# Batch 0's second half of G inside its first FFN steps, batch 1's expert search at step 24, and a plan adapted to both

## The chip, the cores and the metric

One core of one Trainium2 chip. The metric is the device time of one launch in microseconds, median over runs. The core has TensorE for matmuls (PE in the profile, its weight loads PEld), VectorE (DVE), ScalarE (ACT), GpSimd (POOL), and SyncE (SP), whose queue issues nearly all DMA transfers of this kernel. Each engine works through its own queue in order.

## What is computed

Eight batches, eight heads, 576 tokens per batch, head width 64. A packed attention comes first: 32 queries p attend to k and v, and the 32 packed rows then serve as keys and values for q. The output, 4608 rows of 512, goes through a mixture of eight experts, where each row takes its best expert:

```
p_packed = softmax(p k^T / 8) v             # 32 rows per head
x        = softmax(q p_packed^T / 8) p_packed   # rows of 8 heads side by side: 4608 x 512
e        = argmax(x w_gate)                 # per row
out[row] = softmax(x w_gate)[e] * sigmoid(x w_output_gate)[e] * (relu(x w1[e]) w2[e])
```

All arrays are float32. For the inputs drawn, the rows of a batch go to one expert but for a few.

## The kernel before, in words

The kernel works batch by batch, and per batch on one expert, which it finds at run time from the packed rows. Rows that belong to another expert are mended afterwards (`first_leftover`, and a loop that runs zero times here if nothing is left).

For batch b there are five jobs, each a Python generator that emits instructions piece by piece:

- `encode(b)`: scores of p against k on PE (`ps_s`), their maximum (`nm` on DVE; from batch 1 on a relay between ACT and DVE, `top_of`), exponentials on ACT, transposes on DVE, the product with v on PE (`ps_pp`), the packed rows (`ppc`, stored to `pp_d`), their transpose `ppT`, the expert's scores (`ps_e`), and last `find_top`, which leaves the expert's number in `estar_i`. 18 pieces for batch 0, 16 for the others.
- `weights(b)`: SP loads the expert's number into a register (`value_load`) and issues four 512 KB transfers of w1 (tile `w`, line 505); the next piece issues four of w2 (`wst`); then, in turn for each of the four parts of w2, ACT makes a rounded copy `w2h` (L519) and DVE or POOL the remainder `w2l` (L521).
- `values_up(b)`: G = packed rows times w1 on PE (`ps_G`, L99), so that the FFN's first product can be taken from the attention weights directly. G comes in two halves of 512 columns; each half needs two of w1's four parts. A half's PSUM banks are split into `Gh` (ACT, L83) and `Gl` (DVE, L84), for batch 0 in quarters of 256 columns.
- `route(b)`: scores of q against the packed rows (`ps_s2T`), softmax over the packed rows (DVE, ACT, POOL), the attention weights as `ah` (ACT) and `al` (DVE or POOL), stored to `a_d`, then the gate: per-row expert, scale `scm_all`, and a count of the rows that need mending (`keys`).
- `ffn(b)`: yields after each step. Steps 1 to 8: eight column blocks of the first product for the first 256 tokens (`ps_h`, L92, six matmuls each), each taken out by ACT (L577) and DVE (L580) as `hT`. Steps 9 to 16: the second product for those tokens (`ps_o`, L618, twelve matmuls per two steps of work). Steps 17 to 24: the first product for the other 320 tokens. Steps 25 to 27: the second product of the last 64 tokens (L633). Steps 28 to 35: the remaining two blocks of 128 tokens. Column blocks 0 to 3 need only the first half of G. The last batch has three steps more.

Order is written out by hand. `START` is emitted before batch 0's FFN, and `PLANS[b]` says which pieces follow which step of `ffn(b)`: "24:r" puts one piece of `route(b+1)` behind step 24. Letters in capitals and `t`, `W`, `G` mean a job of batch b itself (Y encode, t route, W weights, G values_up), small letters the same job of batch b+1 (y, r, w, g), `x` is encode of batch b+2, `k`, `v`, `q` fetch the next input block, `d` scales and stores the two output blocks that batches 0 and 1 keep back, `l` is the mending, and a digit is `keep_warm`: matmuls on a blank tile. `CFG["warm"]` has their sizes in blocks of 128 columns, and `CFG["pool"]` lists the element-wise steps that go to POOL instead of DVE. An instruction that waits holds up what stands behind it in its engine's queue; SP's queue holds the value loads, all fetches and all stores.

PSUM has eight banks, four named "a" and four named "f". G's first half, `ps_h` and `ps_o` use "f" banks in rotation; a bank is given on when ACT and DVE have taken its contents. The q buffers are two, the k and v buffers six.

Of the kernel before, what the change touches and what calls it, by code (L numbers as in the profile page):

```python
# [18 lines left out]

P = 128  # L20
BANK = 512
CFG = dict(raw=6, rq=2, pa=4, w1=4, wst=4, w2=6, a1T=2, at=2, row=4, ht=4, ob=4, last=(4, 2, 3), warm=(8, 6, 1, 6, 3, 1, 5, 5),
           pool=("w2.2", "w3.3", "w4.3", "w5.3", "w6.3", "w7.3", "w3.0", "w4.0", "w5.0", "w6.0", "w7.0", "w0.0",
# [4 lines left out]

START = "kkYY3YvqYYvk1qYYkYYYY4YYYYYYtYttWt2tqttWk6v7tv5tvqttttvytGGqGG"
STEADY = ("3:yy 5:q 7:k 8:rWryy 9:rryrr 10:r 11:t 12:r 13:rr 14:ry 16:w 17:rw 18:x 19:vx 20:q 21:x 24:vx "
          "26:xrxw 28:wr 29:r 30:kww 31:xgx 33:g 34:rwwxwxg")
PLANS = ["1:W 3:k 4:WW 6:WtW 7:ty 8:W 9:Wy 10:ty 12:W 13:y 14:ttyt 15:ytyy 17:y 18:tyt 19:q 20:y 21:yrry 22:t "
# [5 lines left out]
        + [STEADY] * 4 + ["6:W 7:t 8:l 21:ll 28:l 29:l 30:l 33:l"]  # L41


@with_exitstack
def tile_packed_attn_then_moe(ctx, tc, first_in, qT, kp, k2, v, w1, w2, out):
# [26 lines left out]

    NA = CFG["pa"]

    def bank(name, tag="a"):
        return pool.tile([P, BANK], F32, tag=tag, name=name, bufs=NA if tag == "a" else 8 - NA)
# [40 lines left out]
    def keep_warm(i):  # L117

        ps = bank("warm", "fa"[0 < i < 6])
        n = CFG["warm"][i]  # L120
        while n:
# [21 lines left out]
    no_row = float(2 * B * S)  # L143
    key_i = sb.tile([P, B * T * Q * E], I32, tag="hT", name="key_i", bufs=CFG["ht"], **WIDE)
    nc.gpsimd.iota(key_i, pattern=[[1, B * T * Q * E]], base=0, channel_multiplier=0)
# [46 lines left out]
    def eng(what, *at):  # L192
        return nc.gpsimd if what + ".".join(map(str, at)) in CFG["pool"] else nc.vector

# [10 lines left out]
    def fetch(x):  # L205
# [5 lines left out]
        tag = "rq" if x == "q" else "raw"  # L211
        bufs = CFG[tag]
        if x == "v":
# [29 lines left out]
    def encode(b):  # L243
# [42 lines left out]
        for hf in range(2):  # L286
# [10 lines left out]
            yield  # L297
        a1s = [sb.tile([P, S], F32, tag="row", name="a1", bufs=CFG["row"]) for _ in range(NG)]
        ats = [sb.tile([P, S], F32, tag="a1T", name="a1T", bufs=CFG["a1T"]) for _ in range(NG)]
# [517 lines left out]
    def place(plan, b):  # L817

        kinds = dict(x=(encode, 2), y=(encode, 1), Y=(encode, 0), r=(route, 1), t=(route, 0), w=(weights, 1), W=(weights, 0),
                     g=(values_up, 1), G=(values_up, 0), l=(first_leftover, 0))  # L820
        for c in plan:
            if c in kinds:
                piece(kinds[c][0], b + kinds[c][1])
            elif c == "d":
                store()
            elif c.isdigit():
                keep_warm(int(c))
            else:
                fetch(c)

    by_hand = tc.manual_schedule()
    by_hand.__enter__()
    place(START, 0)
    for b in range(B):
        plan = {}
        for x in PLANS[b].split():
            i, what = x.split(":")
# [13 lines left out]
def _layout(q, k, v, p, moe_w_gate, moe_w_output_gate, moe_w1, moe_w2):  # L851
# [26 lines left out]
    def parts(x):  # L878
        x = x.reshape(P, -1)
        n = x.shape[1] - NPAIR * SQ  # L880
        return [x[:, :n], x[:, n:]]
    queues = dict(k=[parts(kp[0]), parts(k2[0])], v=[[v[0, 0]], [v[0, 1], w_go]], q=[parts(x) for x in qT[0]])
    order = [x for c in START if queues.get(c) for x in queues[c].pop(0)]
    return dict(
# [27 lines left out]
```

## Time and profile before

| | us |
|---|---|
| median of 3 runs | 399.0 (398.81 to 399.13) |
| the profiled execution | 400.09 |
| its span, first to last instruction | 398.5 |
| PE busy | 388.6 (98% of the span) |
| DVE, ACT, POOL busy | 257.8, 185.5, 96.5 |
| mean granted TensorE clock, share of full | 0.993 |
| moved by DMA | 83.77 MB, 210 GB/s over the span |

The profiled execution took 1.6 us more than its span and 1.1 us more than the median of the runs. PE is nearly always busy, so the reading goes to the few places where it isn't, or where what it does is not work of the reference.

### The profile page before, as it was taken

What the parts mean: (1) busy time and instruction counts of PE and PEld (TensorE: products, weight loads), DVE (VectorE), ACT (ScalarE), POOL (GpSimd) and SP (SyncE); (2) the same over time, 40 slices, a digit from 0 to 9 for tenths busy, and PEclk for the clock granted to TensorE, in tenths of its full rate; (3) what the DMA queues carried; (4) which work ended last, traced back from release to release, by engine and by line L of the source; (5) the groups of instructions that cost most, each with busy time, mean ns of one, the idle gap of its engine ahead of it and who ended that gap; (6) DMA issues with size and microseconds to landing.
All of it is one profiled execution on the core that took longest, in us unless ns stands there. A gap on an engine that the chain in (4) does not pass through costs nothing.

```text
span 398.5 us, 9681 instructions
## 1 busy us (share of the span) xinstructions
PE 388.6 (98%) x3787; PEld 311.7 (78%) x3787; DVE 257.8 (65%) x717; ACT 185.5 (47%) x424; POOL 96.5 (24%) x85
## 2 busy tenths in 40 slices
PE   8899998999999999999999999999999999999995
PEld 3468876678869786898868887798968887698875
DVE  5678677685778973567663866469564873568421
ACT  2256444562477262744565336553465343632320
POOL 3441014042026210541044012330135010620010
PEclk9899999999999999999999999999999999999998
DMA  7899079935993499324991369613861049101931
GB/s 294 320 390 383 5 224 313 404 119 211 396 318 139 152 306 400 112 97 148 330 403 45 127 211 386 246 38 108 306 251 61 2 141 375 65 29 27 356 118 53
DMA packets 35534, 83.77 MB, mean 210 GB/s; under 512 B 3486, under 2 KB 15136, under 8 KB 35488
## 3 DMA queue, kind: packets, MB, share of 16 engines
q1 hardware_dynamic: 35024, 81.89, 56.0%
q10 hardware_dynamic: 432, 1.26, 0.8%
q8 instruction: 30, 0.49, 0.5%
q14 instruction: 16, 0.13, 0.1%
q0 software_dynamic: 32, 0.00, 0.0%
HBM read 67.93 MB, written 15.27 MB: 209 GB/s over the span
## 4 chain that ended last, share of the span: by engine, by line
PE 91%; DMA 4%; DVE 2%; ACT 1%; SPq 1%; issue 1%; ACTq 0%
PE ps_o L618 43%; PE ps_h L92 25%; PE ps_o L633 8%; DMA w<-in_w_dram 4%; PE ps_G L99 3%; PE ps_pp L99 3%; PE ps_s L99 2%; PE ps_s2T L99 2%; PE warm L123 2%; PE ps_lg L99 1%; SPq L505 1%; PE ps_lo L778 0%; PE ps_lh L762 0%; DVE nm L290 0%; PE ps_ppT L336 0%
## 5 line engine op out<-in xcount | busy, mean ns | idle before, releaser
L618 PE MATMUL ps_o<-w2h,hT 128*128 128x512 f32 (+2 forms) x528 | 168.0, 390 | 0.0
L618 PEld LDWEIGHTS ps_o<-w2h,hT 128*128 128x128 f32 x528 | 98.5, 188 | 23.3 <-issue 2.8
L618 PE MATMUL ps_o<-w2l,hT 128*128 128x512 f32 (+2 forms) x264 | 101.7, 385 | 0.0
L580 DVE SCALAR_TENSOR_TENSOR hT<-ps_h,hT 128x256 fp32r<-128x256 f32 x192 | 60.6, 352 | 51.0 <-ACT hT L577 50.7
L521 POOL TENSOR_TENSOR w2l<-wst,w2h 128x1024 fp32r<-128x1024 f32 x26 | 63.9, 2467 | 112.0 <-ACT w2h L519 109.1
L92 PE MATMUL ps_h<-ah,Gh 128*128 128x256 f32 (+1 forms) x256 | 77.4, 302 | 0.5 <-DVE Gl L84 0.3
L92 PE MATMUL ps_h<-ah,Gl 128*128 128x256 f32 (+1 forms) x256 | 75.7, 296 | 0.0
L92 PE MATMUL ps_h<-al,Gh 128*128 128x256 f32 (+1 forms) x256 | 75.7, 296 | 0.0
L577 ACT ACTIVATE hT<-ps_h 128x320 fp32r<-128x320 f32 (+1 forms) x128 | 50.9, 416 | 40.9 <-PE ps_h L92 40.5
L618 PEld LDWEIGHTS ps_o<-w2l,hT 128*128 128x128 f32 x264 | 49.7, 188 | 8.7
L92 PEld LDWEIGHTS ps_h<-ah,Gh 128*128 128x128 f32 x256 | 48.6, 190 | 4.1 <-issue 1.2
L92 PEld LDWEIGHTS ps_h<-al,Gh 128*128 128x128 f32 x256 | 48.6, 190 | 0.5
L92 PEld LDWEIGHTS ps_h<-ah,Gl 128*128 128x128 f32 x256 | 48.5, 190 | 0.0
L519 ACT CAST w2h<-wst 128x1024 fp32r<-128x1024 f32 x32 | 33.7, 1061 | 14.3 <-issue 8.5
L84 DVE TENSOR_TENSOR Gl<-ps_G,Gh 128x512 fp32r<-128x512 f32 (+1 forms) x36 | 21.0, 626 | 23.9 <-ACT Gh L83 23.7
L601 ACT ACTIVATE ob<-ps_o,scm_all 128x512 f32<-128x512 f32 (+1 forms) x28 | 19.1, 681 | 33.3 <-PE ps_o L618 31.5
L436 POOL TENSOR_TENSOR al<-a2T,ah 128x576 fp32r<-128x576 f32 (+1 forms) x9 | 11.8, 1317 | 81.5 <-ACT ah L433 81.5
L633 PE MATMUL ps_o<-w2h,hT 128*128 128x512 f32 x64 | 25.8, 403 | 0.0
L633 PE MATMUL ps_o<-w2l,hT 128*64 128x512 f32 x64 | 23.8, 392 | 0.0
L83 ACT CAST Gh<-ps_G 128x512 fp32r<-128x512 f32 (+1 forms) x36 | 17.8, 544 | 7.7 <-PE ps_G L99 7.2
L304 ACT ACTIVATE a<-ps_s,nm 128x144 f32<-128x144 f32 x64 | 18.5, 408 | 4.9 <-DVE nm L273 4.8
L412 ACT ACTIVATE s<-s 128x576 f32<-128x576 f32 (+1 forms) x18 | 11.1, 631 | 20.4 <-DVE s L409 19.0
(177 smaller groups left out, 403.9 us busy)
## 6 DMA issues: line engine op xcount, KB each, us to landing
w<-in_w_dram SPq DMA_DIRECT2D x36, 512.0 KB, 5.9
wst<-in_w_dram SPq DMA_DIRECT2D x36, 512.0 KB, 9.0
vt<-in_v_dram SPq DMA_DIRECT2D x14, 650.0 KB, 10.8
q<-in_qT_dram SPq DMA_DIRECT2D x14, 576.0 KB, 5.2
out_dram<-ob SPq DMA_DIRECT2D x31, 256.0 KB, 2.0
a_d<-a2T SPq DMA_DIRECT2D x16, 320.0 KB, 2.9
k<-in_kp_dram SPq DMA_DIRECT2D x7, 640.0 KB, 8.1
k<-in_k_dram SPq DMA_DIRECT2D x7, 576.0 KB, 7.0
```

Of the source, the lines that this page charges most:

```text
L83: (hi_eng or nc.scalar.copy)(hi, src)
L84: (lo_eng or nc.vector).tensor_tensor(lo, src, f(hi), ALU.subtract)
L92: res = nc.tensor.matmul(dst, a, m, start=j == 0, stop=j == len(seq) - 1)
L99: res = nc.tensor.matmul(dst, a, m, start=j == 0, stop=j == len(seqs[0]) - 1)
L304: nc.scalar.activation(a1s[g][:, c * SQ:(c + 1) * SQ], s1[c // 2][g][:, (c % 2) * SQ:(c % 2 + 1) * SQ], AF.Exp, bias=nm[:, g, c:c + 1], sc ...
L519: nc.scalar.copy(hi, st)
L521: eng("w", b, j).tensor_tensor(lo, st, f(hi), ALU.subtract)
L577: nc.scalar.activation(hT[:, :n], ps, AF.Relu)
L580: nc.vector.scalar_tensor_tensor(hT[:, d0:d0 + s1 - s0], ps[:, s0:s1], 0.0, f(hT[:, s0:s1]), op0=ALU.max, op1=ALU.subtract)
L601: nc.scalar.activation(ob[:, cs], ps[:, cs], AF.Copy, scale=sc)
L618: nc.tensor.matmul(ps[:, cs], a, m[:, cs], start=fc == i == 0, stop=fc == FC - 1 and i == 2)
L633: nc.tensor.matmul(ps[:n], a, m, start=i == 0, stop=i == len(seq) - 1)
```

## The change

Only the plan changes: `START`, `STEADY`, the three own plans of batches 0 to 2, the plan of the last batch, the sizes of the blank matmuls, and the list of steps that go to POOL. No arithmetic changes.

- `START` ends in "GkyG" where it ended in "vytGGqGG": only the first half of G is made ahead of the FFN, with the first piece of batch 1's encode between its matmuls and its split. The second half's matmuls and split stand behind step 2 of batch 0's FFN ("2:GGW").
- In `START` the first piece of `route(0)` (the matmuls `ps_s2T`) moves ahead of the last pieces of `encode(0)`, and the transfers of w2 are issued directly behind those of w1.
- In `PLANS[0]` the last pieces of `encode(1)` (`find_top`) and the search with w1's transfers move to step 24 ("24:yyw"), from steps 29 and 30. The stores `d` move from step 26 to 23. The split of w2 moves from steps 1, 4, 6, 8, 9 and 12 to steps 2, 3, 6, 7, 9 and 10.
- In `STEADY` and the others, pieces shift by one to three steps; among them the relay of `encode(b+2)` goes from step 21 to 23. The first piece of the mending goes from step 8 to 11.
- The blank matmuls go from 8, 6, 1, 6, 3, 1, 5, 5 blocks to 7, 4, 1, 6, 1, 8, 3, 1.

```diff
-CFG = dict(raw=6, rq=2, pa=4, w1=4, wst=4, w2=6, a1T=2, at=2, row=4, ht=4, ob=4, last=(4, 2, 3), warm=(8, 6, 1, 6, 3, 1, 5, 5),
+CFG = dict(raw=6, rq=2, pa=4, w1=4, wst=4, w2=6, a1T=2, at=2, row=4, ht=4, ob=4, last=(4, 2, 3), warm=(7, 4, 1, 6, 1, 8, 3, 1),
            pool=("w2.2", "w3.3", "w4.3", "w5.3", "w6.3", "w7.3", "w3.0", "w4.0", "w5.0", "w6.0", "w7.0", "w0.0",
-                 "w1.2", "w3.2", "w4.2", "w5.2", "w6.2", "w7.2", "mul2.0.0", "sub1.0.1", "w2.1", "w1.1",
-                 "al3.0.1", "al4.0.1", "al5.0.1", "al6.0.1", "al7.0.1", "sub1.0.0", "w3.1", "w4.1", "w5.1",
-                 "w6.1", "w7.1", "al1.0.0", "w2.3", "mul0.0.0", "al0.0.1", "al2.0.0", "sub2.0.1", "sub0.0.1",
-                 "mul0.0.1", "al0.0.0", "mul1.0.1", "sub2.0.0"))
+                 "w1.2", "w3.2", "w4.2", "w5.2", "w6.2", "w7.2", "w2.1", "w1.1", "al3.0.1", "al4.0.1", "al5.0.1",
+                 "al6.0.1", "al7.0.1", "sub1.0.0", "w3.1", "w4.1", "w5.1", "w6.1", "w7.1", "al1.0.0", "al0.0.1",
+                 "sub2.0.1", "al0.0.0", "w2.3", "mul1.0.0", "sub0.0.1", "sub0.0.0", "al2.0.1", "sub2.0.0",
+                 "w0.2", "mul2.0.1", "al2.0.0", "mul0.0.0"))
-START = "kkYY3YvqYYvk1qYYkYYYY4YYYYYYtYttWt2tqttWk6v7tv5tvqttttvytGGqGG"
-STEADY = ("3:yy 5:q 7:k 8:rWryy 9:rryrr 10:r 11:t 12:r 13:rr 14:ry 16:w 17:rw 18:x 19:vx 20:q 21:x 24:vx "
-          "26:xrxw 28:wr 29:r 30:kww 31:xgx 33:g 34:rwwxwxg")
-PLANS = ["1:W 3:k 4:WW 6:WtW 7:ty 8:W 9:Wy 10:ty 12:W 13:y 14:ttyt 15:ytyy 17:y 18:tyt 19:q 20:y 21:yrry 22:t "
-         "24:r 25:r 26:d 27:yt 28:rr 29:yr 30:rw 31:wk 33:r 34:rtkgrgrg",
-         "0:Wyyy 3:W 4:W 5:vyyyyW 6:W 7:W 9:yyWyt 10:yW 11:yt 12:rtt 13:yydr 15:yrry 16:r 17:q 20:q 21:r 22:r "
-         "23:w 24:vx 25:xx 26:rwk 27:rw 28:rvr 30:rt 31:x 32:rrg 33:xrww 34:vwgxwrwg",
-         "0:ky 3:tyyy 5:Wq 6:yy 7:W 8:ryr 9:yr 10:rr 11:rkry 12:rrx 13:xxv 14:xqyrxw 16:wx 17:rx 18:rv 20:kxr "
-         "21:r 26:g 28:r 30:wg 31:gr 32:w 33:xwx 34:wwww"] \
-        + [STEADY] * 4 + ["6:W 7:t 8:l 21:ll 28:l 29:l 30:l 33:l"]
+START = "kkvYY3qYYYvYqYY1kYkYYYYY4YtYYtYtWtWtv2tqvttv7qt5tvt6ttGkyG"
+STEADY = ("3:yy 7:k 8:ryy 9:rrrrW 10:ty 11:qr 12:r 13:r 14:r 15:r 16:yw 17:rrw 18:x 19:v 21:x 23:vx 24:x 25:r "
+          "26:xwx 27:r 28:wx 29:qr 30:wkw 31:gx 33:g 34:rwxwxwg")
+PLANS = ["0:kq 1:t 2:GGW 3:W 5:ty 6:W 7:tW 9:WWW 10:yW 11:tt 12:t 13:y 14:ytyy 15:qt 16:yy 17:y 18:tty 19:y "
+         "21:ryt 22:y 23:dr 24:yyw 25:r 26:r 29:rw 30:tr 31:r 32:rt 33:rr 34:rkgkrgg",
+         "0:Wyyy 4:WW 5:yyyWy 6:vW 7:W 9:Wyyyt 10:yW 11:yt 12:t 13:rydy 15:ytr 16:ryr 17:rq 20:r 21:q 22:v "
+         "23:rwxx 24:wrx 26:kr 27:twr 28:r 29:v 31:xrx 32:rrvg 33:rrw 34:wwgxwwg",
+         "0:yk 2:q 3:ytyy 5:W 6:yy 7:W 8:ryr 9:yxr 10:k 11:rxrry 12:rr 13:rxxqv 14:xyx 16:rrxw 18:wr 20:xr "
+         "23:k 24:vr 28:g 29:r 30:rwg 31:gw 32:www 33:wxx 34:w"] \
+        + [STEADY] * 4 + ["6:W 7:t 11:l 21:ll 29:l 30:l 31:l 34:l"]
```

## Rows read from the trace of the kernel before

**Rows 1.** Idle PE time from 24 us on: who waited for whom, us, times, longest.

```profile
PE ps_G L99 <- DMA w<-in_w_dram: 1.6, 3, 1.2
PE ps_h L92 <- DVE Gl L84: 0.3, 1, 0.3
PE ps_h L92 <- DVE hT L580: 0.3, 1, 0.3
```

**Rows 2.** The chain that ended last: start us, us, what, times.

```profile
17.42 7.46 DMA w<-in_w_dram
...
26.05 0.36 ACT Gh L83
...
27.30 0.44 DVE Gl L84
...
27.88 4.54 PE ps_h L92 x36
32.42 10.90 PE ps_o L618 x48
...
54.16 3.67 PE ps_o L633 x16
...
63.45 7.58 DMA w<-in_w_dram
...
206.18 1.88 PE ps_G L99 x32
...
290.97 1.12 PE ps_o L633 x4
```

**Rows 3.** Timeline to 30 us: start, us, engine, line, operation, count [idle before, releaser].

```profile
15.30 1.20 PE L99 MATMUL ps_s2T<-q,ppT 64*32 64x288 f32 x32
...
17.53 4.38 PE L123 MATMUL warm<-blank 128*128 128x128 f32 x12 [1.03 <-issue]
...
21.83 1.24 PE L99 MATMUL ps_s<-k 64*32 64x144 f32 x64
22.24 1.79 POOL L436 TENSOR_TENSOR al<-a2T,ah 128x288 fp32r<-128x288 f32 x2 [0.43 <-ACT ah L433]
...
22.84 1.89 PE L99 MATMUL ps_G<-w,ppT 64*32 64x512 f32 x24
...
25.91 0.39 PE L92 MATMUL ps_h<-ah,Gh 128*128 128x256 f32 x1
```

**Rows 4.** DMA issues around 16.4 us, w1's second part: size, us to landing.

```profile
w<-in_w_dram SPq DMA_DIRECT2D x1, 512.0 KB, 5.0
```

**Rows 5.** Page, part 5, w2's rounded copy: count, busy us, mean ns, idle before.

```profile
L519 ACT CAST w2h<-wst 128x1024 fp32r<-128x1024 f32 x32 | 33.7, 1061 | 14.3 <-issue 8.5
```

**Rows 6.** Timeline, 56 to 82 us: batch 1's search, its G, its first FFN step.

```profile
59.95 0.56 SPq L640 DMA_DIRECT2D out_dram<-ob  x1
...
61.36 2.43 SPq L505 DMA_DIRECT2D w<-in_w_dram  x4
...
67.51 1.09 PE L99 MATMUL ps_G<-w,ppT 64*32 64x512 f32 x16
...
70.52 0.75 DVE L436 TENSOR_TENSOR al<-a2T,ah 128x576 fp32r<-128x576 f32 x1
...
72.08 0.19 PEld L618 LDWEIGHTS ps_o<-w2h,hT 128*128 128x128 f32 x1 [0.84 <-issue]
...
74.85 0.19 PEld L92 LDWEIGHTS ps_h<-ah,Gh 128*128 128x128 f32 x1 [0.23 <-issue]
```

**Rows 7.** Busy us of each engine by stretch (instructions), granted clock, DMA share, GB/s.

```profile
17.20:20.60 3.40, 3.07 (x7) 2.03 (x8) 2.89 (x9) 0.89 (x2) 0.76 (x2) 0.50 0.94 341
...
25.90:43.30 17.40, 17.14 (x104) 14.78 (x104) 14.29 (x34) 12.56 (x33) 2.86 (x3) 1.00 0.79 318
...
206.20:251.90 45.70, 45.70 (x459) 37.51 (x467) 29.64 (x83) 23.15 (x52) 11.38 (x7) 1.00 0.58 217
```

**Rows 8.** ACT's timeline in batch 5, the take-outs behind the relay.

```profile
288.05 1.09 ACT L577 ACTIVATE hT<-ps_h 128x320 fp32r<-128x320 f32 x3
```

## The prediction

> **What bounds the kernel now.** I read the waits of PE first. From 24 us on it stands idle in three places only, all before 80 us: G waits for w1's transfers, and two steps of the FFN wait for DVE [rows 1]. After that the busy time by stretch shows PE full: a whole batch of the steady plan takes 45.70 us with 45.70 us of PE [rows 7]. So PE's own work is the bound from 80 us to the end, and nothing that the change shifts there can win anything. It can win only in the start (to 26 us) and in batch 0. The chain of waits gives the unit prices: a `ps_h` matmul of 256 columns 4.54 us / 36 = 0.126, a `ps_o` matmul 10.90 / 48 = 0.227, a whole G 1.88 us when nothing holds it up, one quarter's `Gh` 0.36 and `Gl` 0.44 [rows 2].
>
> **Term 1, the search for batch 1.** G of batch 1 starts at 67.51 and PE comes back to `ps_o` at 72.08 [rows 6]: 4.57 us for 1.88 us of matmuls [rows 2]. The other 2.69 us are the wait for w1, whose last transfer was issued at 63.45 and landed at 71.03 [rows 2]. It was late because SP's value load stood behind the store of the 64-token block at 59.95 [rows 6], which waits for step 27's product to be taken out. The change emits the search behind step 24, ahead of that block's product, which starts at 54.16 [rows 2]. Then SP has in front of it only the two stores of `d`, which move to step 23 with it, and `find_top` on DVE. I take the first transfer 5 us earlier, 61.36 - 5 = 56.4 (an estimate from 54.16 plus about 2 us for DVE's queue and the load; bounds 55.2 and 58.5). The issue of the four takes 2.43 us, its last part starts 2.1 us in, and the last landing takes 7.58 us as before: 56.4 + 2.1 + 7.6 = 66.1 (64.9 to 68.2). The last quarter of G's matmuls needs it 1.4 us after G's start, at 68.9, or 68.4 with term 2. All 2.69 us go, and at the late bound too. What is late next: `al` of batch 1 is done at 70.52 + 0.75 = 71.27, and the FFN, which started at 74.85 [rows 6], would now start at 74.85 - 2.7 - 0.5 = 71.65. Its margin is 0.4 us, and on DVE it stood behind `Gl`, which comes earlier too, so I charge nothing; bound 0.5 us. The wait of `ps_h` for `hT` in batch 1 (0.3 [rows 1]) hangs on the relay at step 0, which stays. Moved along: w2's four issues to step 29, the stores `d`, the two count pieces; all were late against no one in these rows.
>
> **Term 2, the start.** The first FFN matmul stands at 25.91 [rows 3]. Before it PE does blank matmuls (17.53 to 21.9), batch 1's scores (21.83, 1.24 us), then G in the order of w1's landings, the last at 17.42 + 7.46 = 24.88 [rows 2, 3]. The first half of G needs only w1's second part, issued at 16.36 and landed 5.0 us later at 21.4 [rows 4]. The change makes that half directly behind the blank matmuls, puts the scores behind it, and leaves the second half out. So G's first half runs from about 21.4 for 0.94 us; then one `Gh` and two `Gl` (0.36 + 2 x 0.44, and some 0.1 between) give 23.7. The other input is `al`, done at 22.24 + 1.79 = 24.03 [rows 3]. Its chain begins with `ps_s2T` at 15.30, which the change moves ahead of a matmul that waited for a copy; it can start some 0.7 us earlier, so `al` comes at about 23.3. I take the first FFN matmul at 23.9, 2.0 us earlier. Bounds: 23.7, and 25.3 if G's first half still runs at 22.84 and only the second half's time is saved.
>
> What is paid back: 0.94 us of G inside the FFN, and ACT. Between steps 0 and 8 ACT has eight take-outs (about 0.39 each), four `Gh` (1.45), two `w2h` at 1.06 [rows 5] and two exponentials (0.8): 7.4 us against 48 x 0.126 + 0.94 = 7.0 us of PE. Four "f" banks are the slack, and a `w2h` now stands ahead of the take-out of block 2. I estimate 0.5 us of wait at blocks 4 and 6, and 0.5 us when the product reaches w2's second part, whose copy moves from step 4 to 6. The old wait, 0.43 us from 27.45 to 27.88 [rows 2], goes, since fewer banks are tied up in G at step 1. First FFN matmul to the end of `ps_o` was 43.32 - 25.91 = 17.41; it becomes 17.41 + 0.94 + 1.0 - 0.43 = 18.9. So term 2 is 2.0 - 1.5 = 0.5 us won. Bounds: 2.2 - 0.94 + 0.43 = 1.7 won with no wait, 0.6 - 1.5 = 0.9 lost with the late start.
>
> The blank matmuls cost nothing in either version as long as they end before 21.4; their count behind the search goes from 12 blocks to 13.
>
> POOL takes a subtract and one more `w2l` from DVE. DVE is 14.29 us busy of 17.40 between 25.90 and 43.30 [rows 7], so that relief is inside the waits above. The Trainium skill (SBUF — State Buffer, Who interferes with whom) says that a GpSimd step and a DVE step with two SBUF inputs exclude each other for a whole instruction, which speaks against handing such steps to POOL. By it the wait of 0.5 us at w2's second part would be nearer to a microsecond; no row here shows that pair.
>
> **Term 3, the rest.** Steady batches have no PE idle, the same PE work before and after, and their pieces shift by a few steps: 0, bounds +0.4 and -0.2. The mending moves one step (about 1.4 us) later at its end, and PE has some 8 us of `ps_o` behind it: 0.
>
> **Sum.** 2.7 + 0.5 = 3.2 us. The profiled execution would go from 400.09 (span 398.5) to 396.9 (395.3). It stood 1.1 us above the median of the runs, 399.0, so the median should come to 395.8. Likeliest case alone: 394.8 to 397.0.
>
> **Rivals.**
>
> First, the start gives nothing or costs. One mechanism is TensorE's clock: the granted clock is 0.50 between 17.2 and 20.6, the lower of its two levels, after PE stood idle for 1.03 us [rows 3, 7]. There it slows blank matmuls only. If the drop comes 3 us later, because the idle time before it is cut and the blank matmuls end earlier, a stretch as long as that one falls on G and the first FFN blocks, and half of its 3.4 us is lost: 1.7 us, so 397.5. Against it: nearly as many blank blocks stand in the same place. The Trainium skill (TensorE: Matmul & The Clock Gate, What's actually happening) calls the half rate the default that activity lifts; the rows agree, and do not tell when it falls next. The other mechanism is the late start and the ACT waits, 0.9 us lost: 397.2. Together 18%.
>
> Second, the search is emitted earlier but not done earlier. SP waits at the fetch of q for batch 2 until `ps_s2T` of batch 1 has run, at about 50 us in both versions, and two stores of `a_d`, `pp_d`, another q and `d` stand between. If those hold the load until 61, the wait of 2.69 us stays: 399.0 - 0.5 = 398.5, no change that can be told. For it: DVE's queue lags PE there. Against it: by term 1 the load may come 2.5 us later than I take it and still end the wait. 8%.
>
> Third, slower: the steady plan. The relay of `encode(b+2)` goes from step 21 to 23, two blocks of 0.88 us later. Behind it the last three take-outs ended at 288.05 + 1.09 = 289.14 on ACT [rows 8], DVE adds some 0.8, and the part of the product that needs the last of them starts at 290.97 [rows 2]. 289.9 + 1.76 = 291.7 is 0.7 us late. Only block 7 is now behind the relay, not three, which takes about 0.9 us off and leaves 0.2 us of room. If the relay also holds the exponentials or DVE's queue in between, each of four batches and perhaps batch 6 loses the same; from 0.8 us per batch on it outweighs terms 1 and 2. With 1.2 us each, four batches cost 4.8: 400.6. 10%.
>
> **How the numbers follow.** Forecast 395.8, 62%; first rival 397.2 to 397.5, 18%; second 398.5, 8%; third 399.5 to 401, 10%; something better than the forecast's own range, 2%. The range 394.4 to 398.5 holds the forecast, the first rival and the bounds of term 2; the third lies outside. A measurement of this kernel can tell about 0.2%, 0.8 us. Faster than 398.2: 62 + 18 + 2 = 82%, of which I move 1 to the middle, where the second rival lies: 81%; within 0.2%: 9%; slower: 10%.
>
> **What would show it.** Right: w1 of batch 1 issued before 59 us, G of batch 1 in about 1.9 us without a DMA wait, the first `ps_h` near 24 us, `ps_G` again behind block 1, and a steady batch of 45.7 us. Wrong: a `ps_G` wait that stays, the first `ps_h` after 25.5, the granted clock at 0.50 after 21.4, waits of `ps_h` on `hT` in steps 1 to 8 above 1.0 us in sum, or a steady batch above 46 us.

## The result

| | before | changed |
|---|---|---|
| median, us | 399.06 (4 runs, 398.81 to 399.41) | 395.27 (4 runs, 395.17 to 395.52) |
| ratio, 95% interval | | 0.9896 (0.9878 to 0.9914) |
| the profiled execution, us | 400.09 | 395.52 |
| its span, us | 398.5 | 393.9 |
| mean granted TensorE clock | 0.993 | 0.998 |

The forecast was 395.8 (394.4 to 398.5). The medians differ by 3.8 us, the two profiled executions by 4.57: the one of before stood 1.03 above its median, the one of the change 0.25. The ratio on record, 0.9896, is not that of these two medians (0.9905); its interval, 3.4 to 4.9 us, holds both. The changed kernel, run a second time beside some of the experiments, gave 0.9893 (0.9873 to 0.9913). Where an experiment's ratio is turned into microseconds below, it is (ratio - 1) x 399.

The start of the changed kernel, as in [rows 3] (timeline: start, us, engine, line, operation, count, idle before):

```profile
17.52 2.85 PE L123 MATMUL warm<-blank 128*128 128x128 f32 x8 [1.53 <-DVE s L393]
...
20.31 1.26 PE L99 MATMUL ps_G<-w,ppT 64*32 64x512 f32 x16
...
20.94 1.81 POOL L436 TENSOR_TENSOR al<-a2T,ah 128x288 fp32r<-128x288 f32 x2 [1.05 <-ACT ah L433]
21.19 1.38 PE L99 MATMUL ps_s<-k 64*32 64x144 f32 x64
21.63 0.64 ACT L83 CAST Gh<-ps_G 128x256 fp32r<-128x256 f32 x2
22.03 1.62 DVE L84 TENSOR_TENSOR Gl<-ps_G,Gh 128x256 fp32r<-128x256 f32 x4
...
22.50 0.39 PE L92 MATMUL ps_h<-ah,Gh 128*128 128x256 f32 x1
...
24.12 1.33 PE L99 MATMUL ps_G<-w,ppT 64*32 64x512 f32 x16
```

The first FFN matmul comes at 22.50, where it stood at 25.91 [rows 3]. G's first half starts as soon as the blank matmuls end, and its second half stands behind two FFN blocks. That half needs two transfers of w1; the later of them, as in [rows 4] (size, us to landing), took 4.3 us where it had taken 5.0:

```profile
w<-in_w_dram SPq DMA_DIRECT2D x1, 512.0 KB, 4.3
```

Batch 1's search and its G, as in [rows 6]:

```profile
54.26 0.17 DVE L355 FIND_INDEX8 estar_i<-e_top,ps_e 128x8 uint32<-128x8 f32 x1
...
55.83 2.43 SPq L505 DMA_DIRECT2D w<-in_w_dram  x4
...
58.41 0.57 SPq L640 DMA_DIRECT2D out_dram<-ob  x1
...
65.89 1.95 PE L99 MATMUL ps_G<-w,ppT 64*32 64x512 f32 x32
...
70.88 0.39 PE L92 MATMUL ps_h<-ah,Gh 128*128 128x256 f32 x1
```

w1 is asked for at 55.83 instead of 61.36, now ahead of the store of the 64-token block, and G has no gap in it. From 24 us to the end of the FFN the list of waits names no idle time of PE at all, where [rows 1] had 2.2 us. The chain of waits, as in [rows 2]:

```profile
22.57 1.63 PE ps_h L92 x12
24.19 1.26 PE ps_G L99 x16
25.45 1.27 PE ps_h L92 x9
26.74 3.77 PE ps_h L92 x27
30.50 11.01 PE ps_o L618 x48
...
65.96 1.88 PE ps_G L99 x32
...
201.66 1.88 PE ps_G L99 x32
```

And by stretch, as in [rows 7] (busy us of PE, PEld, DVE, ACT, POOL with instructions, granted clock, DMA share, GB/s):

```profile
17.20:20.60 3.40, 3.08 (x16) 1.53 (x24) 2.16 (x7) 0.86 (x3) 1.08 (x2) 1.00 1.01 375
22.50:41.40 18.90, 18.89 (x116) 15.20 (x112) 15.93 (x37) 13.42 (x35) 5.88 (x5) 1.00 0.95 383
201.60:247.30 45.70, 45.70 (x458) 37.51 (x460) 29.69 (x82) 22.77 (x51) 11.30 (x7) 1.00 0.60 217
```

A steady batch is what it was. The clock, 0.50 in the first of these stretches before, was at 1.00 throughout.

So the 4.57 us between the two profiles split like this. At the end of batch 0's first `ps_o` (32.42 + 10.90 = 43.32 by [rows 2], 30.50 + 11.01 = 41.51 now) the change leads by 1.8. At the start of G of batch 1 (67.51 by [rows 6], 65.89) it leads by 1.62, at its end (72.08, 67.77) by 4.31: the wait gives 2.69. At the first FFN matmul of batch 1 (74.85, 70.88) it is 3.97, at G of batch 2 (116.10, 111.60 in the two chains) 4.5, and at G of batch 4 (206.18, 201.66) still 4.5.

### The profile page after: what moved, and what is told of

Its sections match the earlier page's. It is cut to its first block, busy times and chain, and to the rows that moved or that the text cites. A ratio compares the mean times of both kernels' runs of the same rounds, so it can differ in the third digit from the quotient of the medians.

```text
span 393.9 us, 9676 instructions
## 1 busy us (share of the span) xinstructions
PE 384.8 (98%) x3783; PEld 311.1 (79%) x3783; DVE 256.7 (65%) x716; ACT 184.8 (47%) x424; POOL 98.9 (25%) x86
## 3 DMA queue, kind: packets, MB, share of 16 engines
q10 hardware_dynamic: 432, 1.26, 0.8%
## 4 chain that ended last, share of the span: by engine, by line
PE 95%; DVE 2%; DMA 1%; ACT 0%; issue 0%; ACTq 0%
PE ps_o L618 46%; PE ps_h L92 26%; PE ps_o L633 8%; PE ps_G L99 4%; PE ps_pp L99 3%; PE ps_s L99 3%; PE ps_s2T L99 2%; PE ps_lg L99 1%; PE warm L123 1%; DMA k<-in_first_dram 1%; PE ps_lo L778 0%; PE ps_lh L762 0%; DVE s L393 0%; PE ps_ppT L336 0%; DVE a1T L317 0%
## 5 line engine op out<-in xcount | busy, mean ns | idle before, releaser
L521 POOL TENSOR_TENSOR w2l<-wst,w2h 128x1024 fp32r<-128x1024 f32 x27 | 66.7, 2480 | 98.2 <-ACT w2h L519 95.2
L436 POOL TENSOR_TENSOR al<-a2T,ah 128x576 fp32r<-128x576 f32 (+1 forms) x10 | 13.2, 1320 | 96.2 <-ACT ah L433 94.1
```

The source lines that it names most:

```text
L521: eng("w", b, j).tensor_tensor(lo, st, f(hi), ALU.subtract)
```

## The experiments

### The search alone

The kernel before with only the search and the stores `d` moved:

```diff
-         "24:r 25:r 26:d 27:yt 28:rr 29:yr 30:rw 31:wk 33:r 34:rtkgrgrg",
+         "23:d 24:ryyw 25:r 27:t 28:rr 29:r 30:r 31:wk 33:r 34:rtkgrgrg",
```

> The kernel before with one part of the change alone: the last two pieces of encode(1), the search and w1's transfers go to step 24, and d to step 23; start, other batches and POOL list as before. Theory (the search takes 2.7 us off the wait of G of batch 1, whatever the start does): 396.4, with G of batch 1 in about 1.9 us and w1 issued near 57 to 58 us. Rival (the load is held by what stands ahead of it on SP, and the gain of the change comes from the start): 398.8 to 399.2.

Measured: 0.9979 (0.9955 to 1.0002), 0.8 us less, nearer to the rival's time than to the theory's; the interval reaches to no change at all. Its chain of waits and its issue of w1 (timeline):

```profile
55.13 0.24 DVE scm_all L482
...
55.46 1.34 ACT ob L597 x2
56.80 0.33 ACT hT L577
...
57.15 0.57 DVE hT L580 x2
...
67.95 2.81 PE ps_G L99 x32
```

```profile
60.08 2.44 SPq L505 DMA_DIRECT2D w<-in_w_dram  x4
```

Emitted at step 24, the search was done only 1.3 us earlier (60.08 for 61.36), since DVE had the gate of batch 0 in front of it: `scm_all` at 55.13, which the change has at 51.35. `find_top` ended at 58.8 there, at 60.2 in the kernel before, at 54.4 in the change. And the scaling for `d`, moved to step 23 but waiting for that same `scm_all`, held ACT for 1.34 us ahead of a take-out that PE's next product needed; DVE's part of that take-out, which stood ahead of `find_top`, waited with it. G still lasted 0.9 us too long (2.81 against 1.88). So the search was moved together with batch 0's pieces in front of it, as the change does:

```diff
-PLANS = ["... 20:y 21:yrry 22:t "
-         "24:r 25:r 26:d 27:yt 28:rr 29:yr 30:rw 31:wk 33:r 34:rtkgrgrg",
+PLANS = ["... 20:y 21:ryt 22:y "
+         "23:dr 24:yyw 25:r 26:r 29:rw 30:tr 31:r 32:rt 33:rr 34:rkgkrgg",
```

> The kernel before with batch 0's pieces from step 21 on put where the change has them: the search of batch 1 at 24 and also the transpose and gate pieces ahead of it earlier (the run with the search alone moved left them and gave 0.998). Theory (the first matrix of batch 1 comes late because the search waits for the gate piece ahead of it on the vector engine; with that moved too the matrix is asked for at 57.5 or sooner): G of batch 1 without a DMA wait, 2.5 us less than the kernel before, ratio 0.9935 to 0.9945. Rival (the order on the queues decides nothing, the engines' work up to there does): request not before 59.5, ratio 0.997 to 1.

```profile
52.37 0.22 DVE L482 SCALAR_TENSOR_TENSOR scm_all<-idx_all,estar_all,scale_all 128x5 f32<-128x5 f32 x1
...
57.82 2.44 SPq L505 DMA_DIRECT2D w<-in_w_dram  x4
...
66.91 1.95 PE L99 MATMUL ps_G<-w,ppT 64*32 64x512 f32 x32
```

Measured: 0.9956 (0.9940 to 0.9972), 1.8 us less. The mechanism is the theory's: with the gate at 52.37 w1 is asked for at 57.82, 0.3 us later than the latest expected, and G has no wait. The size is short of the 2.5 expected; only the edge of the interval reaches the expected ratios. In its chain the scores behind G (`ps_s`) next wait for the split of G (`Gl` on DVE): from the end of G to the first FFN matmul it takes 3.2 us (68.79 to 72.00), where it took 2.8 [rows 6].

### The change without the search

```diff
-         "21:ryt 22:y 23:dr 24:yyw 25:r 26:r 29:rw 30:tr 31:r 32:rt 33:rr 34:rkgkrgg",
+         "21:ryt 22:y 23:dr 25:r 26:r 27:y 29:ry 30:trw 31:wr 32:rt 33:rr 34:rkgkrgg",
```

> The changed kernel with the search put back: the last two pieces of encode(1) at steps 27 and 29, search and w1's transfers at step 30, w2's at 31. Theory (the wait of G of batch 1 returns, 2.7 us, perhaps less as fewer transfers stand ahead): 397.6 to 398.1. Rival (in the changed plan w1 is early enough in any case, because k of batch 2 is fetched before the queue is held up): 395.3 to 395.8.

```profile
59.95 2.42 SPq L505 DMA_DIRECT2D w<-in_w_dram  x4
...
65.40 1.23 PE L99 MATMUL ps_G<-w,ppT 64*32 64x512 f32 x16
...
67.49 2.25 PE L99 MATMUL ps_G<-w,ppT 64*32 64x512 f32 x16 [0.86 <-DMA w<-in_w_dram]
```

Measured: 0.9946 (0.9928 to 0.9964), 2.2 us less, where the theory had 1.0 to 1.5 less and the rival 3.3 to 3.8. The time lies between them, nearer to the theory's, and the mechanism is the theory's: the wait of G is back (65.40 to 69.74, 4.3 us for 1.88 us of matmuls), and with it about 2 us of the gain. What is left is mainly the start, and it is worth more than I had expected. The search with the gate (1.8) and the rest alone (2.2) add up to 4.0; the whole change gives 4.1 to 4.3.

### The second half of G, alone and left out

The kernel before with only the split of G:

```diff
-START = "... tvqttttvytGGqGG"
+START = "... tvqttttvytGGq"
-PLANS = ["1:W 3:k 4:WW ...
+PLANS = ["1:W 2:GG 3:k 4:WW ...
```

> The kernel before with the other named part alone: the matmuls and the split of G's second half go from ahead of the FFN to behind step 2; order of the start and blank matmuls as before. Theory (the start wins by its new order, in which G's first half comes right behind the blank matmuls, and not by moving the second half alone): first FFN matmul near 25.3, 0.6 us earlier, 0.94 us and some waits paid inside the FFN: 398.9 to 399.5. Rival (taking the second half out of the way is what wins the start): 397.5 to 398.

Measured: 1.0034 (1.0014 to 1.0055), 1.4 us more. Both expectations missed. Its stretch of 17.2 to 20.6 us by engine and clock, and its start:

```profile
17.20:20.60 3.40, 2.52 (x6) 1.49 (x7) 2.91 (x9) 0.89 (x2) 0.74 (x2) 0.50 0.94 329
```

```profile
18.08 5.49 PE L123 MATMUL warm<-blank 128*128 128x128 f32 x12 [1.57 <-issue]
23.50 1.24 PE L99 MATMUL ps_s<-k 64*32 64x144 f32 x64
24.51 1.09 PE L99 MATMUL ps_G<-w,ppT 64*32 64x512 f32 x16
```

The granted clock was 0.50, the lower of its two levels, from 16.69 to 23.52, and the blank matmuls, 4.38 us long in [rows 3], took 5.49. They ended 2.3 us after the second transfer that G's first half needs had landed (at 21.2); G, behind the scores, started at 24.51, and the first FFN matmul came at 26.09. The time hardly follows the clock, though: the four executions with a mean clock of 0.997 to 0.999 took 400.3 to 401.8 us, the other eight 400.2 to 402.4. My next theory was therefore that the split pays once no blank matmul stands in front of G. Two runs, with the last two groups of blanks cut, with and without the split:

```diff
-... warm=(8, 6, 1, 6, 3, 1, 5, 5),
+... warm=(8, 6, 1, 6, 3, 1, 1, 1),
```

> The kernel before with the second half of batch 0's G behind the first FFN blocks, as in the earlier run with that alone, and with the last two groups of blank matmuls cut from 5 to 1 each. In the earlier run the blanks ran at half clock until 23.57 us, 2.4 us after the second part of the first matrix had landed, and the split gained nothing (1.003). Theory (the split is worth its earlier start as soon as no blank stands in front of G): first FFN matmul at 22.5 to 23.7, of the 2.2 to 3.4 us some 1.6 are paid back by G's second half in the FFN and the clock, ratio 0.9955 to 0.998. Rival (the order of the start's pieces, not the blanks, is what the split needs): ratio 0.9995 to 1.0035.

> The kernel before, G whole ahead of the FFN, with the same two groups of blank matmuls cut from 5 to 1. Theory (with all of G ahead, the last part of the first matrix, which lands at 24.9, sets the first FFN matmul, and neither blanks nor the half clock do): first FFN matmul at 25.2 to 26, ratio 0.998 to 1.001. Rival (blanks and clock set it): first FFN matmul at 24.5 or sooner, ratio 0.995 to 0.9965.

With the split: 1.0038 (1.0026 to 1.0049), 1.5 us more. The theory's time did not come, but the rival's, and a little above it. Without it: 0.9995 (0.9983 to 1.0006), as its theory had it. In that run the clock was at 0.50 for 6.8 us, and it made no difference, because w1's last part decides (PE, timeline):

```profile
24.85 1.06 PE L99 MATMUL ps_G<-w,ppT 64*32 64x512 f32 x8 [0.38 <-DMA w<-in_w_dram]
...
25.84 0.38 PE L92 MATMUL ps_h<-ah,Gh 128*128 128x256 f32 x1
```

What holds the split back in the old order is read from the run with the split and few blanks. Its profiled execution ran 2.86 us later from the start on (`ps_s2T` at 18.16, 15.30 in [rows 3]), so its times are to be read with that taken off. The first FFN matmul then stands at 23.1, 2.8 us earlier than before, where the theory had wanted it. It is paid back behind: from there to the end of `ps_o` it takes 21.4 us (25.98 to 47.33), against 17.4 in the kernel before, 18.8 in the run with the split alone and 19.0 in the change. PE, then DVE, then ACT:

```profile
25.98 0.39 PE L92 MATMUL ps_h<-ah,Gh 128*128 128x256 f32 x1 [1.35 <-ACT Gh L83]
...
27.58 0.39 PE L92 MATMUL ps_h<-ah,Gl 128*128 128x256 f32 x1 [1.09 <-DVE Gl L84]
...
25.12 0.41 DVE L408 TENSOR_REDUCE mx<-s 128x9 f32<-128x288 f32 x1
25.56 0.65 DVE L409 TENSOR_TENSOR s<-s,mx 128x288 f32<-128x288 f32 x1
26.14 0.44 DVE L408 TENSOR_REDUCE mx<-s 128x9 f32<-128x288 f32 x1
26.61 0.57 DVE L409 TENSOR_TENSOR s<-s,mx 128x288 f32<-128x288 f32 x1
27.11 1.61 DVE L84 TENSOR_TENSOR Gl<-ps_G,Gh 128x256 fp32r<-128x256 f32 x4
...
30.25 1.05 ACT L519 CAST w2h<-wst 128x1024 fp32r<-128x1024 f32 x1 [1.52 <-DMA wst<-in_w_dram]
31.20 0.38 ACT L577 ACTIVATE hT<-ps_h 128x256 fp32r<-128x256 f32 x1
```

G's matmuls are no longer late, but their split is. The old `START` has one piece of `route(0)`, the beginning of the softmax for the next 256 tokens, ahead of G: 2.0 us of DVE (25.12 to 27.11) in front of `Gl`. In the kernel before it lies there too, and ends just before w1's last part lands, so it was free:

```profile
23.77 0.58 DVE L409 TENSOR_TENSOR s<-s,mx 128x288 f32<-128x288 f32 x1
24.40 1.62 DVE L84 TENSOR_TENSOR Gl<-ps_G,Gh 128x256 fp32r<-128x256 f32 x4
```

With the split it became a wait of PE. A second one is `W` at step 1: ACT waits 1.52 us for w2's transfer, with the take-out of block 2 queued behind it; in all PE waited 1.1 us for `hT` there. The change moves both: that softmax piece to step 1, `W` to step 2, w2's transfers directly behind w1's. That these two pieces are what the split needed moved is read from the traces; no run moved them alone.

The counterpart, the changed kernel with all of G ahead of the FFN:

```diff
-START = "... tvt6ttGkyG"
+START = "... tvt6ttGkyGGG"
-PLANS = ["0:kq 1:t 2:GGW 3:W ...
+PLANS = ["0:kq 1:t 2:W 3:W ...
```

> The changed kernel with G's second half put back ahead of the FFN, behind the split of the first; all else as changed. Theory (PE then waits for w1's last part, which lands at 24.4 us, before its first FFN matmul: that goes from 22.5 to about 25.4, of which some 1.3 us come back because no G stands inside the FFN): 396.6 to 397.2. Rival (what is won ahead is paid back inside, the place of the second half is neutral): 395.1 to 395.6.

```profile
24.70 1.06 PE L99 MATMUL ps_G<-w,ppT 64*32 64x512 f32 x8 [0.66 <-DMA w<-in_w_dram]
25.69 0.38 PE L92 MATMUL ps_h<-ah,Gh 128*128 128x256 f32 x1
```

Measured: 0.9926 (0.9897 to 0.9956), 3.0 us less, against 4.1 to 4.3 with the split; the interval is too wide to tell the two expectations apart by time. The profile does: the first FFN matmul is back at 25.69, although the new order is there and the clock is at 1.00 throughout the start, and the last `ps_o` starts at 390.93, 1.6 us behind the change's 389.32. Two of the eight executions took the change's time (395.3 and 395.7), the others 397.2 to 398.0; what set the two apart is not known. So the new order with all of G ahead gives the start almost nothing (0.2 us at the end of `ps_o`, 43.11 against 43.32), the split in the old order costs 1.4 us, and the two together give 1.8 us. The split brings the first FFN matmul forward once no blanks hold G up, and the new order keeps PE from waiting behind it.

### Blank matmuls and clock

> The changed kernel itself once more, as the common measure for the three runs beside it. If both theories about the start are looked at with fair numbers, it should stand at 0.990 to 0.9915 of the kernel before (395.3 against 399.06 so far), the start's clock without a drop, first FFN matmul near 22.5 us, G of batch 1 without a DMA wait.

```diff
-... warm=(7, 4, 1, 6, 1, 8, 3, 1),
+... warm=(8, 6, 1, 6, 3, 1, 5, 5),
```

> The change with the numbers of blank matmuls of the kernel before, the plan as in the change. Theory A (the start's gain of some 1.3 us over what was forecast comes from the clock that did not fall, and what the clock does hangs on the blanks): the clock falls somewhere between 16 and 24 us, first FFN matmul 23.5 or later, 396.2 to 397.0. Theory B (the order of the pieces made the start earlier, the blanks are only filling): first FFN matmul near 22.5, 395.1 to 395.6.

```diff
-... warm=(7, 4, 1, 6, 1, 8, 3, 1),
+... warm=(7, 4, 1, 6, 1, 1, 1, 1),
```

> The change with the last four groups of blank matmuls cut from 1, 8, 3, 1 to one each, so that the tensor engine idles while it waits for the first half's softmax and the first matrix. Theory A: the idle time is followed by a stretch at 0.5 of the clock over G and the first FFN blocks, 396.3 to 397.2. Theory B: nothing is lost, or the start even gets earlier since no blank stands ahead of G, 394.9 to 395.5.

Measured, on one chip: the change 0.9893 (0.9873 to 0.9913), the blanks of before 0.9908 (0.9887 to 0.9929), few blanks 0.9916 (0.9896 to 0.9935), with medians of 395.05, 395.85 and 396.22 us. The intervals overlap; the change came out a little below the 0.990 expected of it, the other two between theory A's times and theory B's. In all three profiles the clock is at 1.00 in the start, and the first FFN matmul comes at 22.08, 22.80 and 22.24. The order of the pieces makes the start early (theory B in the profiles). But the runs with few blanks fall apart by their clock: 395.2 and 395.5 at a mean of 0.998 to 1.000, 396.2 to 396.9 in the four at 0.991 to 0.992; with the blanks of before two of six took 396.3 and 396.95, at 0.995 and 0.993. That looks like theory A in some executions; no profile caught one, so it is not shown.

### The steady plan and the POOL list

Both are the change with one part as before: `STEADY` and the last plan, and the list `pool`.

> The change with the steady plan of batches 3 to 6 and the last batch's plan of the kernel before. Theory (these plans are worth nothing: TensorE is busy throughout a steady batch of 45.7 us in both): the ratio of the change, 0.9885 to 0.991. Rival (the moved pieces gain or cost a wait in each steady batch): 0.4 us a batch, 1.6 in all, ratio below 0.9865 or above 0.993.

> The change with the list of the operations on the slow vector-like engine (GpSimd) of the kernel before. Theory (they hang on the start's engines only where al0 and sub0 wait there, and cost at most 0.3 us): first FFN matmul within 0.4 us of 22.5, ratio 0.989 to 0.992. Rival (the change's start is early only because of what lies on which engine): first FFN matmul 23.2 or later, ratio 0.992 to 0.996.

The steady plan of before: 0.9914 (0.9893 to 0.9935), a hair above the theory's 0.991 and short of the rival's 0.993; it does not differ from the change, and by its stretch a steady batch takes the same 45.70 us:

```profile
201.60:247.30 45.70, 45.70 (x459) 37.49 (x451) 29.87 (x83) 23.35 (x53) 11.46 (x8) 1.00 0.59 220
```

The POOL list of before: 0.9904 (0.9887 to 0.9922), the theory's time too. Its profiled execution has the first FFN matmul where the rival had it, at 23.55, but for another reason: the clock fell in the start, the only one among eight profiles with the new `START`.

```profile
17.94:21.35 3.41, 3.41 (x5) 1.02 (x4) 2.31 (x7) 0.86 (x2) 1.99 (x3) 0.50 0.99 376
```

```profile
17.02 4.55 PE L123 MATMUL warm<-blank 128*128 128x128 f32 x8 [1.54 <-DVE s L393]
21.50 1.09 PE L99 MATMUL ps_G<-w,ppT 64*32 64x512 f32 x16
...
23.55 0.39 PE L92 MATMUL ps_h<-ah,Gh 128*128 128x256 f32 x1
```

The blanks took 4.55 us instead of 2.85, G began at 21.50 instead of 20.31, the first FFN matmul came at 23.55 instead of 22.50, still 2.4 us earlier than in the kernel before. The execution took 396.6; the other four of this kernel 395.5 to 395.9.

## Why the prediction was right, step by step

**Term 1 was right in mechanism and size.** w1 was asked for at 55.83 (56.4 taken, 55.2 to 58.5 the bounds), its last part landed at about 65.1 (66.1), and G lost exactly the 2.69 us of wait. Without the search about 2 us of the gain go. Its reason for the old lateness covers only the last 0.3 us, though: when the store at 59.95 went out, `find_top` itself was not done; it ended on DVE at 60.2. And what the step did not say is that emitting the search earlier is not enough: DVE's queue had the gate in front of it, and the run with the search alone kept most of the wait. My second rival was this mechanism, placed on SP; the change escapes it because the gate moves too. The stretch between G and the first FFN matmul, whose margin I charged at nothing, did cost 0.34 us (4.31 to 3.97). It was not `al`, which was done at 66.7; the scores behind G waited for `Gl` on DVE.

**Term 2 failed in one of its two sizes.** What is paid back was right: first FFN matmul to the end of `ps_o` took 41.51 - 22.50 = 19.0 us, 18.9 had been worked out. Its parts were not quite those: G's second half cost 1.26, not 0.94; of the two waits of 0.5 us the first came, as gaps too short for the list (0.2 us more than usual ahead of the matmuls at 26.74 and 27.25, 0.1 ahead of those at 27.47 and 29.03), and the second did not: w2's second part cost 0.1 (`ps_o` 11.01 against 10.90 [rows 2]). The Trainium skill (SBUF — State Buffer, Who interferes with whom) has a DVE step with two SBUF inputs contend with a GpSimd step that reads SBUF. One row of the changed kernel agrees: GpSimd's `w2l` at 32.29, started beside DVE's own `w2l` (31.74 to 32.96), took 2.92 us, the one at 28.09 took 2.41. PE paid no more for it than that 0.1, and no run isolates it.

The mis-sized term is the start: 3.4 us earlier, where 2.0 was taken and 2.2 was the bound. Of the 1.4 us between 23.9 and 22.50, 1.1 lie in the start of G's first half, which I put at 21.4, when its transfer had landed in the profile of before. It came at 20.31: the transfer landed after 4.3 us, not 5.0 [rows 4], at 20.5, and the blank matmuls ended at 20.3, not at 21.9, as the clock did not fall. I had also put all of that half behind the later of its two transfers, while its first eight matmuls need only the earlier one: with all of G ahead they ran at 19.76, and the next at 21.21, after a wait for the DMA. I had said that they cost nothing as long as they end before 21.4; in the run with the old POOL list, with the clock down, they did hold G. From G's start to the first FFN matmul it took 2.2 us as worked out (2.3).

**Term 3** was 0 and came to about nothing in the steady batches. The two bits of batch 0's second half and of batch 1's G (0.19 and 0.34 lost) are outweighed by some 0.5 us that appears within batch 1, between its first FFN matmul and G of batch 2 (3.97 to 4.5). The wait of `ps_h` for `hT` in batch 1 [rows 1], which the listing no longer names, is part of that; what the rest is was not settled, and the plans of batches 1 and 2 were not run alone.

**The sum:** 2.7 + 0.5 + 0 was forecast; the profiles show 2.69 + 1.8 + 0.1 = 4.6. As the execution of before was the slower one against its median, the medians moved by 3.8, and the forecast came out 0.5 us too high. That it came so near is in part luck: the profiled execution was forecast 1.4 us too high (396.9 for 395.52), and the 1.1 us taken off for the median was 0.85 more than the change's own 0.25.

**The rivals.** The first one's clock did not fall later, it did not fall in this kernel's two profiles at all; where it fell in the new order, it cost 1.05 us of the start, not the 1.7 that I had worked out for it. The second did not happen, for the reason given. The third did not happen: the relay at step 23 leaves PE 45.70 us busy of 45.70.

## What to carry to other kernels

Moving an instruction up in the program moves it up only as far as the slowest queue in front of it lets it: list what stands ahead of it on every engine that feeds it (here DVE's gate before SP's load), and move that too. A step that is free while it hides behind a transfer becomes a wait as soon as that transfer is no longer the last to arrive, so a split of work that waits for data has to come with a new order of what used to fill the wait; neither half alone brought anything here. And take the landing time of a transfer and the clock of the start as ranges, not as the one value that a single profile happens to show.

## What the runs showed of the hardware

- The granted clock fell to 0.50 for 3.4 or 6.8 us in the first 24 us in all six profiles with the old `START`, and in one of eight with the new one. Not every execution of the old one can have had it: 16 of the 71 of the kernel before that ran beside the experiments have a mean clock of 0.997 or more, where 3.4 us at half rate would leave at most 0.996 (an estimate, 1 - 1.7 / 398). Idle time ahead of it does not tell these apart: before, PE idled 1.03 us and the clock fell [rows 3, 7]; in the changed kernel it idled 1.53 us at the same place and stayed at 1.00, and with the old POOL list it idled 1.54 us and the clock fell. The Trainium skill (TensorE: Matmul & The Clock Gate, What's actually happening) has activity lift the rate; these rows agree with that, and do not show what in the new order keeps it up. That is left open.
- What the drop costs hangs on what it falls on: nothing that the profiles show where a transfer decides (25.84 for the first FFN matmul with 6.8 us at half rate, 25.91 with 3.4), 1.05 us where the blank matmuls stand ahead of G. Over the runs of the kernel before some half a microsecond may hang on it all the same: the median is 399.2 us for those 16 executions and 399.8 for the 39 with a mean clock of 0.995 or less.
- The same 512 KB transfer, w1's second part, took 5.0 us to land in the profile of before and 4.3 in that of the change, and 5.0 again in the run with all of G ahead, whose start is the change's up to there.
